# Keys transposed on TensorE instead of by DMA, weight words joined in two VectorE steps, and diagonal copies cut to their 32x32 blocks

## The chip, the cores and the metric

The kernel runs on one core of a Trainium2 chip. The metric is device time in microseconds (us) of one execution; the number to forecast is the median of a few executions of the changed kernel. Five engines work side by side, each through its own list of instructions in a fixed order: TensorE (PE, with its weight loads as PEld), VectorE (DVE), ScalarE (ACT), GpSimd (POOL) and SyncE (SP). SP does no arithmetic here: it issues nearly all transfers, in order, and an instruction of it that waits holds back every transfer behind it.

## The reference

Two stages. First a delta rule with a state of 48x48 per head, over 4 batches, 8 heads and 768 positions:

```python
k_n = k / (np.linalg.norm(k, axis=-1, keepdims=True) + 1e-06)
for t in range(S):
    kt, vt, bt = (k_n[:, :, t], v[:, :, t], beta[:, :, t, None])
    y[:, :, t] = np.einsum('bhd,bhde->bhe', q[:, :, t], state)
    v_old = np.einsum('bhde,bhd->bhe', state, kt)
    state = state + bt[:, :, :, None] * np.einsum('bhd,bhe->bhde', kt, vt - v_old)
```

Then a feed-forward layer over the 3072 tokens of 384 numbers that come out, with 2048 hidden units and a rational function:

```python
h = x @ w_in
P = a[0] + a[1] * h + a[2] * h2 + a[3] * h3          # h2 = h*h, h3 = h2*h
Q = 1.0 + np.abs(b[0]) * np.abs(h) + np.abs(b[1]) * h2
return (P / (Q + 1e-06)) @ w_out
```

`moe_w_in` and `moe_w_out` arrive as 64-bit floating-point numbers, two 32-bit words each.

## The kernel before

The 768 positions are cut into 12 chunks of 64. Within a chunk the recurrence is solved in closed form: products of keys with keys (`pg`), an inverse of a triangular matrix by 16x16 blocks on VectorE (`inverse`), and a solve in four steps (`solve_start`, three `solve_step`). Each of the 12 chunks then gives 256 tokens, and the hidden units are worked through in 8 units of 256 (`hidden`, `numerator`, `quotient`, `accumulate`), so there are 96 units in all. Numbers are split into two 16-bit parts, and a product is three passes over them.

The main loop (L1067) goes over the 96 units; beside unit n it runs one slice of attention: `back` of chunk c+1, `middle` of c+2, `front` of c+3, `ahead` of c+4. So the attention of later chunks is hidden under the units of earlier ones. Ahead of the loop stands a start (L1046): the attention of the first chunks, and the loading and conversion of all weights. A scheduler sets the order on each engine from this program and from the buffers; the order is then fixed.

What the change touches:

- **Weights.** `to_f32` (L387) turns a tile of 64-bit words into 32-bit floats. A transfer brings 128x512 (or 128x384) words into one of nine staging buffers (`wsi`, `wso`); ACT takes the absolute value of the high words (L394, tile `wai` or `wao`); POOL clamps it from both sides (L395); DVE shifts it left by 3 and masks it (L396), joins the sign bits of the high word (L403) and the top three bits of the low word (L403 again). That is done for 24 tiles of `w_in` (256 columns) and 32 of `w_out` (192 columns). For `w_out` the lower clamp on POOL is `gate`, a number that DVE makes at the end of the inverse of chunk 0 (L661), so that these tiles come behind that chunk.
- **Keys.** `keys_normalized` (L565) scales a chunk's keys; `transposed` (L526) splits them on POOL into `kn` (L251, L257). For chunk 0 they are transposed on PE (`ptk`, L547) and copied out by ACT in four pieces (L549). For the other 11 chunks `kn` is written to DRAM (`xdk`, L537) and read back by a transposing transfer (`tk`, L554). `xdk` is also what `knbd` is later filled from (L506). Heads are padded from 48 to 64 rows.
- **Diagonals.** A product for two batches at once takes a block-diagonal operand of 128x128 per head: `kbd`, `qbd`, `knbd`, `wbd`, `ebd`, `mbd`. `to_diagonal` (L500) fills its two 64x64 blocks by two transfers of 64 rows. `wbd` serves two things in turn: the triangle `gl` for the product `pe` (L1003, L677), then the inverse `wc` for the solve (L678), so its second filling (L517) waits until PE has done `pe`.
- **Relays through DRAM.** The key products `g` go out to `gd` (L597) and their 16x16 blocks come back as `gb` (L607); the inverse goes out to `img` (L666) and comes back as `wc` (L670), whole 64x64 squares each.
- **PSUM.** The pool `ps_f` has one buffer, which the products of the front stage (`pg`, `pm`, `pe`, `ptq`, `px` and small ones) take in turn.

## Time and profile before

| | us |
|---|---|
| three runs | 833.64, 830.17, 834.09 (median 833.64) |
| the profiled execution, time | 831.25 |
| its span, first to last instruction | 829.5 |
| mean granted TensorE clock | 0.917 |

The profiled execution is 2.4 us under the median, and its own time is 1.75 us more than its span. Busy times of the engines, and how they change over the span, stand in the prediction. In the rows of groups the columns are: source line, engine, operation, output and inputs, shapes, count, then busy us in all and mean ns of one, then the engine's idle time just before and what ended it. Instructions on DVE overlap by some 0.07 us at their ends, so that a duration of 0.25 costs less than 0.25 where another one follows at once.

### The profile page before, as it was taken

Reading aid. Unit: us, or ns where it says so; the run is one execution under the profiler, and the core shown is the slowest. Engines: PE = TensorE matmul, PEld = TensorE weight load, DVE = VectorE, ACT = ScalarE, POOL = GpSimd, SP = SyncE. Lnnn points to the kernel's source line nnn. Section 1 sums busy time; section 2 is a strip of 40 time slices with the busy share of each in tenths; the row PEclk is TensorE's granted clock in tenths of the full one; section 3 lists DMA queues with packets and bytes.
Section 4 is the critical chain, followed back from the end, with each engine's and each line's share of the span. In section 5 each row is a group of like instructions: output and inputs, shape, how many; then the busy total and the mean of one; then the engine's idle time right before and its main releaser. Section 6 shows DMA issues by size and latency. Waiting matters only on the chain.

```text
span 829.5 us, 23311 instructions
## 1 busy us (share of the span) xinstructions
PE 626.5 (76%) x9466; PEld 498.2 (60%) x9466; DVE 752.7 (91%) x1325; ACT 553.8 (67%) x988; POOL 428.0 (52%) x416
## 2 busy tenths in 40 slices
PE   0320445867779678898887898996988979998995
PEld 0210444656568467677666676775766867876663
DVE  5999899878999789899899998989999998997996
ACT  4756666745757466767686776866767766776773
POOL 8653865424261353573664665736735545353532
PEclk9975565898989899999999999998999999999999
DMA  8999897759865777849979468586676733400000
GB/s 231 239 195 197 203 183 139 131 99 165 140 119 105 124 134 125 143 81 147 140 126 155 79 137 149 87 161 116 105 151 101 129 63 55 78 2 20 1 21 19
DMA packets 430956, 99.42 MB, mean 120 GB/s; under 512 B 408064, under 2 KB 427520, under 8 KB 430848
## 3 DMA queue, kind: packets, MB, share of 16 engines
q1 hardware_dynamic: 428672, 96.77, 63.0%
q8 instruction: 74, 1.21, 0.6%
q10 hardware_dynamic: 2176, 1.17, 0.5%
q14 instruction: 34, 0.28, 0.1%
HBM read 40.47 MB, written 19.94 MB: 73 GB/s over the span
## 4 chain that ended last, share of the span: by engine, by line
DVE 44%; PE 16%; issue 11%; DMA 11%; ACT 7%; SPq 6%; POOL 5%; POOLq 0%; DVEq 0%; ACTq 0%
PE ph L867 6%; PE po L929 5%; DVE mw L909 4%; DVE mu L887 4%; DVE mw L889 4%; DVE mu L891 4%; DVE w_out L403 4%; DVE mg L908 3%; DMA q_b<-in_q_dram 3%; DVE mu L913 2%; POOL mg L914 2%; PE pu L479 1%; DVE mg L906 1%; ACT mu L884 1%; DVE z L259 1%
## 5 line engine op out<-in xcount | busy, mean ns | idle before, releaser
L867 PE MATMUL ph<-xT,w_in 128*128 128x256 f16 x1728 | 222.4, 280 | 20.5 <-DVE mu L891 16.7
L929 PE MATMUL po<-w_out,mg 128*128 128x384 f16 x1152 | 218.5, 333 | 24.2 <-POOL mg L914 22.2
L914 POOL TENSOR_TENSOR mg<-mu,mr 128x512 f16<-128x512 f32 x96 | 132.3, 1378 | 154.4 <-DVE mu L913 99.2
L867 PEld LDWEIGHTS <-w_in 128*128 128x128 f16 x1728 | 169.7, 100 | 58.4 <-DVE mu L891 14.0
L929 PEld LDWEIGHTS <-mg 128*128 128x128 f16 x1152 | 108.6, 100 | 93.6 <-POOL mg L914 29.8
L890 ACT ACTIVATE mw<-mw 128x512 f32<-128x512 f32 x96 | 60.4, 629 | 65.0 <-DVE mw L889 64.8
L884 ACT ACTIVATE mu<-ph,coef,msc 128x512 f32<-128x512 f32 x96 | 73.9, 770 | 33.5 <-PE ph L867 19.7
L909 DVE SCALAR_TENSOR_TENSOR mw<-mw,msc,mg 128x512 f32<-128x512 f32 x96 | 89.9, 937 | 0.6
L887 DVE TENSOR_TENSOR mu<-ph,mu 128x512 f32<-128x512 f32 x96 | 65.4, 681 | 24.2 <-ACT mr L886 13.3
L479 PEld LDWEIGHTS <-kbd 128*128 128x128 f16 x1680 | 60.7, 104 | 26.7 <-issue 15.1
L911 POOL TENSOR_TENSOR mu<-mu,mw 128x512 f32<-128x512 f32 x36 | 49.3, 1370 | 48.4 <-DVE mw L909 34.8
L891 DVE SCALAR_TENSOR_TENSOR mu<-mu,msc,ph 128x512 f32<-128x512 f32 x96 | 70.6, 736 | 0.0
L889 DVE SCALAR_TENSOR_TENSOR mw<-mr,msc,ph 128x512 f32<-128x512 f32 x96 | 70.6, 735 | 0.0
L902 ACT ACTIVATE mr<-mw,msc 128x512 f32<-128x512 f32 x96 | 69.1, 720 | 1.6
L886 ACT ACTIVATE mr<-ph,msc 128x512 f32<-128x512 f32 x96 | 65.2, 679 | 0.0
L479 PE MATMUL pu<-z,ebd 128*128 128x48 f16 x1728 | 51.5, 185 | 15.5 <-DVE z L259 13.7
L479 PEld LDWEIGHTS <-ebd 128*128 128x128 f16 x1728 | 50.8, 98 | 18.9 <-issue 15.5
L903 ACT ACTIVATE mr<-mr 128x512 f32<-128x512 f32 x96 | 60.4, 629 | 1.4
L908 DVE SCALAR_TENSOR_TENSOR mg<-mu,msc,mr 128x512 f16<-128x512 f32 x60 | 56.4, 941 | 4.1 <-ACT mr L903 4.1
L479 PEld LDWEIGHTS <-wbd 128*128 128x128 f16 x1152 | 33.9, 99 | 29.1 <-issue 28.5
L895 POOL TENSOR_SCALAR mu<-mu,msc 128x512 f32<-128x512 f32 x36 | 30.9, 858 | 36.9 <-DVE mu L891 34.8
L913 DVE SCALAR_TENSOR_TENSOR mu<-mu,msc,mw 128x512 f32<-128x512 f32 x60 | 49.2, 820 | 0.4
(211 smaller groups left out, 1228.5 us busy)
## 6 DMA issues: line engine op xcount, KB each, us to landing
wsi<-in_moe_w_in_dram SPq DMA_DIRECT2D x24, 256.0 KB, 4.8
xdk<-kn SPq DMA_DIRECT2D x24, 256.0 KB, 3.9
kbd<-tk SPq DMA_DIRECT2D x24, 256.0 KB, 4.6
gd<-g SPq DMA_DIRECT2D x24, 256.0 KB, 4.2
wso<-in_moe_w_out_dram SPq DMA_DIRECT2D x32, 192.0 KB, 3.7
mbd<-mm SPq DMA_DIRECT2D x24, 256.0 KB, 5.0
wc<-img SPq DMA_DIRECT2D x24, 256.0 KB, 4.6
wbd<-wc SPq DMA_DIRECT2D x24, 256.0 KB, 4.4
```

Source lines behind the costliest of these rows:

```text
L479: nc.tensor.matmul(dst[p][:, h], head(bd, lp, p * H + h), head(rt, rp, p * H + h), start=start and n == 0 and h == 0, stop=stop and n == l ...
L867: nc.tensor.matmul(ph[:, i], w_in[:, f2, wp, cc, i * P : (i + 1) * P], x[:, xp, cc], start=k == 0, stop=k == 3 * NCC - 1,)
L884: nc.scalar.activation(u, ph, AF.Identity, scale=A3, bias=a2)
L887: nc.vector.tensor_mul(u, ph, u)
L889: nc.vector.scalar_tensor_tensor(out=w, in0=z, scalar=B0, in1=ph, op0=ALU.add, op1=ALU.mult)
L891: nc.vector.scalar_tensor_tensor(out=u, in0=u, scalar=A1, in1=ph, op0=ALU.add, op1=ALU.mult)
L902: nc.scalar.activation(r, w, AF.Ln, bias=Q0)
L908: nc.vector.scalar_tensor_tensor(out=g[:, 0], in0=u, scalar=A0, in1=r, op0=ALU.add, op1=ALU.mult)
L909: nc.vector.scalar_tensor_tensor(out=w, in0=w, scalar=Q0, in1=g[:, 0], op0=ALU.add, op1=ALU.mult)
L913: nc.vector.scalar_tensor_tensor(out=u, in0=u, scalar=A0, in1=w, op0=ALU.add, op1=ALU.subtract)
L914: nc.gpsimd.tensor_mul(g[:, 1], u, r)
L929: nc.tensor.matmul(po[p], g[:, gp, i, p * P : (p + 1) * P], w_out[:, f2, wp, i], start=f2 == lo and i == 0 and k == 0, stop=f2 == hi - 1 a ...
```

## The change

1. `to_f32` has no masking step and no clamp. ACT takes the absolute value of the high word times a constant (or times `gate`) as a 32-bit float; POOL makes the bare sign bit straight from the high word (minimum with 0, times 0) and writes it to the target `t`; DVE then joins in two steps: low word shifted right by 29, or `t`; absolute value shifted left by 3, or `t`. `gate` moves from POOL's instruction to ACT's.
2. All chunks' keys are transposed on PE: 16 transposes into one `ps_f` buffer (`pk`), and two ACT copies of 96x1024. `xdk` and the transposing transfer are gone, and `knbd` is filled straight from the split keys in SBUF (now called `nk`). The padding of heads from 48 to 64 is gone, so `kbd`, `qbd` and `tk` have 96 rows instead of 128, in transfers of 48 rows instead of 64.
3. `gd`, `wc` and `wbd` are moved as the two 32x32 blocks on the diagonal of each 64x64 square (four transfers of 32 rows in place of two of 64), `mbd` as the 32-row halves of its triangle (four transfers, two of 128 and two of 64 columns). `wc` becomes one fixed buffer, zeroed once by DVE.
4. The triangle `gl` has a diagonal buffer of its own, `gbd` (DVE zeroes it at the start), without its first 16 rows; it no longer shares with `wbd`.

```diff
-        nc.scalar.activation(a, wh.bitcast(F32), AF.Abs)
-        nc.gpsimd.tensor_scalar(a, a, 3.0e38, keep, op0=ALU.min, op1=ALU.max)
-        nc.vector.tensor_scalar(
-            t, a.bitcast(U32), 3, KEEP, op0=ALU.logical_shift_left, op1=ALU.bitwise_and
-        )
-        for word, scalar, in1, op0, op1 in (
-            (wh, 0xC0000000, t, ALU.bitwise_and, ALU.bitwise_or),
-            (wl, 29, t, ALU.logical_shift_right, ALU.bitwise_or),
-        ):
-            nc.vector.scalar_tensor_tensor(out=t, in0=word, scalar=scalar, in1=in1, op0=op0, op1=op1)
+        nc.scalar.activation(a, wh.bitcast(F32), AF.Abs, scale=bias)
+        nc.gpsimd.tensor_scalar(t.bitcast(F32), wh.bitcast(F32), 0.0, 0.0, op0=ALU.min, op1=ALU.mult)
+        for word, scalar, op0 in ((wl, 29, ALU.logical_shift_right), (a.bitcast(U32), 3, ALU.logical_shift_left)):
+            nc.vector.scalar_tensor_tensor(out=t, in0=word, scalar=scalar, in1=t, op0=op0, op1=ALU.bitwise_or)
...
-                for a in range(HG):
+                for p in PAIRS:
                     nc.sync.dma_start(
-                        out=bd[sl].rearrange("t p i (n a) b d -> t (p i n) a b d", a=HG)[:, :, a, b],
-                        in_=t[:, :, :, :, a, b].rearrange("p i n t d -> t (p i n) d"),
+                        out=bd[sl, p, :, :, b].rearrange("t i n d a -> t (i n) (d a)"),
+                        in_=t[p * C : (p + 1) * C, :, :, b].rearrange("t i n d a -> t (i n) (d a)"),
                     )
...
+            elif nm == "g":
+                sl = slice(b * C + 16, (b + 1) * C)
+                nc.sync.dma_start(out=bd[sl, :, b], in_=t[sl])
             elif nm == "w":
-                nc.sync.dma_start(out=bd[sl, :, b, : t.shape[2]], in_=t[sl])
+                for x in HALVES:
+                    nc.sync.dma_start(out=bd[rows_of(b, x), :, b, x], in_=t[rows_of(b, x), :, x])
             else:
-                nc.sync.dma_start(out=bd[sl, :, :, b, : t.shape[3]], in_=t[sl])
+                for x in HALVES:
+                    nc.sync.dma_start(
+                        out=bd[rows_of(b, x), :, :, b, x.start :], in_=t[rows_of(b, x), :, :, x.start :]
+                    )
...
-        for p in PAIRS:
-            nc.sync.dma_start(
-                out=xd[p].rearrange("i n t a b d -> t (i n) (a b d)"),
-                in_=x[p * C : (p + 1) * C].rearrange("t i (n a) b d -> t (i n) (a b d)", n=NH),
+        pt = ps_f.tile([P, 2, NPAIR, H, C], F16, tag="a", name="p" + nm)[:R]
+        t = sb.tile([R, 2, NPAIR, NH, C, HG], F16, tag="tt", name="t" + nm)
+        for i in range(2):
+            for h in range(H):
+                n, a = divmod(h, HG)
+                nc.tensor.transpose(
+                    pt[:, i, :, h], x[:, i, n, :, :, a].rearrange("p b d -> p (b d)"), ident16
+                )
+            nc.scalar.copy(
+                t[:, i].rearrange("x p n t a -> x (p n) a t"), pt[:, i].rearrange("x p (n a) t -> x (p n) a t", a=HG)
             )
...
-        nc.sync.dma_start(
-            out=t.rearrange("x p i n t a -> x (p i n t a)"),
-            in_=xd.rearrange("p i n t a b d -> (p i n t a) (b d)"),
-            transpose=True,
-        )
...
-            nc.sync.dma_start(out=as_rows(gd, b), in_=g[b * C : (b + 1) * C])
+            for t in HALVES:
+                nc.sync.dma_start(out=as_rows(gd, b)[t, :, t], in_=g[rows_of(b, t), :, t])
...
-            nc.sync.dma_start(out=words[b * C : (b + 1) * C], in_=as_rows(im, b))
+            for t in HALVES:
+                nc.sync.dma_start(out=words[rows_of(b, t), :, t], in_=as_rows(im, b)[t, :, t])
...
-                info[c]["gbd"] = to_diagonal("w", info[c].pop("gl"))
+                info[c]["gbd"] = to_diagonal("g", info[c].pop("gl"))
```

The scheduler's order moves with it. First, VectorE at the first weight tiles. `wai` is what ACT and POOL have made of a tile, `wsi` the tile as it landed, `w_out` the memory in which the float is put together. Before:

```order
L396 TENSOR_SCALAR w_out<-wai_0_790 128x256
L403 SCALAR_TENSOR_TENSOR w_out<-wsi_0_788,w_out 128x256 x2
L396 TENSOR_SCALAR w_out<-wai_1_798 128x256
L403 SCALAR_TENSOR_TENSOR w_out<-wsi_1_796,w_out 128x256 x2
L396 TENSOR_SCALAR w_out<-wai_2_806 128x256
```

And now:

```order
L394 SCALAR_TENSOR_TENSOR w_out<-wsi_0_792,w_out 128x256
L394 SCALAR_TENSOR_TENSOR w_out<-wai_0_794,w_out 128x256
L394 SCALAR_TENSOR_TENSOR w_out<-wsi_1_799,w_out 128x256
L394 SCALAR_TENSOR_TENSOR w_out<-wai_1_801,w_out 128x256
L394 SCALAR_TENSOR_TENSOR w_out<-wsi_2_806,w_out 128x256
```

Three instructions on a tile have become two, and the first of them no longer reads what ACT makes.

Second, SyncE behind the end of the inverse of chunk 0, whose result is `wh` and goes to `img`. Before:

```order
L666 DMA img_147<-wh_383 128x16x16
L554 DMA_TRANSPOSE tk_1558<-xdk_1555 128x2048
L670 DMA wc_388<-img_147 64x16x64 x2
L391 DMA wso_1_1211<-in_moe_w_out_dram 128x384
L391 DMA wso_0_1220<-in_moe_w_out_dram 128x384
```

After seven more tiles of `w_out` there came `kbd`, and only then `wbd`. Now:

```order
L653 DMA img_147<-wh_382 128x16x16
L516 DMA mbd_143<-mm_375 32x16x128
L516 DMA mbd_143<-mm_375 32x16x64
L516 DMA mbd_143<-mm_375 32x16x128
L658 DMA wc_127<-img_147 32x16x32 x4
L513 DMA wbd_139<-wc_127 32x16x64 x4
L516 DMA mbd_143<-mm_375 32x16x64
L388 DMA wso_1_1182<-in_moe_w_out_dram 128x384
```

The next tile of `w_out` (the tenth) now stands behind `wbd`, which waits until `wc` has landed; before, it stood behind `wc` alone.

Third, ScalarE in the main loop, around the square of chunk 8's `v` (`sq_8`). `mu` and `mr` are a unit's first two activations out of PSUM, `mw` its third. Before:

```order
L886 ACTIVATE mr_7557<-ph_7536,msc_6417 128x512
L255 ACTIVATE z_1_7833<-pu_7572,zmask 128x768
L267 ACTIVATE sq_8_7889,fs_7886<-v_7399 128x768
L890 ACTIVATE mw_7506<-mw_7506 128x512
L613 COPY wt_129<-bblk 128x16
```

And now:

```order
L875 ACTIVATE mr_7631<-ph_7610,msc_6521 128x512
L264 ACTIVATE sq_8_8020,fs_8017<-v_7527 128x768
L542 COPY tk_7177<-pk_7176 96x8x2x64
L556 ACTIVATE sq_8286<-k_7754 128x768
L879 ACTIVATE mw_7634<-mw_7634 128x512
L542 COPY tk_7177<-pk_7176 96x8x2x64
```

The two copies out of the new transposes stand between the activations of a unit, one on each side of `mw`.

More of the change, by code (lines that the diff above doesn't have):

```diff
@@ L57 @@
     C = 64
-    DP = 64
+    R = 2 * D
     NB = C // 16
@@ L108 @@
     SRC = {"k": k, "q": q, "v": v}
-    LD_BUFS = {"k": 1, "v": 2}
+    LD_BUFS = {"k": 1, "q": 1, "v": 2}
     loaded = {}
     def load(nm, c):
-        if nm == "q":
-            t = q_b
-        else:
-            t = sb.tile([P, NPAIR * H, D], F32, tag="ld" + nm, name=f"{nm}_{c}", bufs=LD_BUFS[nm])
+        t = sb.tile([P, HP, D], F32, tag="ld" + nm, name=f"{nm}_{c}", bufs=LD_BUFS[nm])
         with behind(nm, c):
@@ L122, in load @@
                 else:
+                    part = t[sl].rearrange("t (h i) d -> t h i d", i=2)
                     for i in range(2):
-                        if nm == "q":
-                            nc.sync.dma_start(out=t[sl, :, i, :D], in_=src[2 * i + b].rearrange("h t d -> t h d"))
-                            continue
-                        nc.sync.dma_start(out=t[sl, i * H : (i + 1) * H], in_=src[2 * i + b].rearrange("h t d -> t h d"))
+                        nc.sync.dma_start(out=part[:, :, i], in_=src[2 * i + b].rearrange("h t d -> t h d"))
         loaded[nm, c] = t
-    q_b = cpool.tile([P, H, 2, DP], F32, name="q_b")
-    nc.vector.memset(q_b[..., D:], 0.0)
     identf = cpool.tile([P, P], F32, name="identf")
@@ L217 @@
             nm + "bd",
-            eng=nc.vector if nm in "kwe" else nc.gpsimd,
+            eng=nc.vector if nm in "kweg" else nc.gpsimd,
         )
@@ L240, in as_rows, with rows_of @@
         )
+    HALVES = [slice(i * C // 2, (i + 1) * C // 2) for i in range(2)]
+    def rows_of(b, t):
+        return slice(b * C + t.start, b * C + t.stop)
     def as_blocks(ap):
         return ap[:, : 16 * C].rearrange("m (i s) -> m i s", s=C)[:, :, :16]
-    S16 = cpool.tile([P, HP, D], F32, name="S16")
+    S16 = cpool.tile([R, HP, D], F32, name="S16")
     def split16(dst, src, scale=None, eng=None, hi=None):
@@ L457, in head @@
         elif t.shape[3] == NH and t.shape[-1] == HG:
-            t = t[:, p, part, h // HG, ..., h % HG]
+            t = (t[:, p, part] if t.shape[-2] == D else t[:, part, p])[:, h // HG, ..., h % HG]
         elif t.shape[2] == HP:
             t = t[:, part, m]
-        elif t.shape[3] == H:
-            t = t[:, p, part, h]
         else:
@@ L476, in mm3p @@
     def mm3p(dst, bd, rt, p, start=True, stop=True):
+        out = R if bd is diag["kn"][0] else 2 * (C - 16) if bd is diag["g"][0] else P
+        rows = R if any(bd is t for t in diag["q"] + diag["k"]) else P
         for n, (lp, rp) in enumerate(PASSES):
@@ L479, in mm3p @@
                 nc.tensor.matmul(
-                    dst[p][:, h],
-                    head(bd, lp, p * H + h),
-                    head(rt, rp, p * H + h),
+                    dst[p][:out, h],
+                    head(bd, lp, p * H + h)[:rows],
+                    head(rt, rp, p * H + h)[:rows],
                     start=start and n == 0 and h == 0,
@@ L524, in grouped, with transposed @@
         return t.rearrange("p (g a) x -> p g a x", a=HG)
-    def transposed(x, src, nm, soon):
+    def transposed(src, nm):
+        x = sb.tile([P, 2, NH, 2, D, HG], F16, tag="kn", name="n" + nm, bufs=3)
         split16(
-            [x[:, i, :, :, :D].rearrange("p h b d -> p b h d") for i in range(2)],
-            src.rearrange("p (b h) d -> p b h d", b=2),
+            [x[:, i].rearrange("p n b d a -> p n a (b d)") for i in range(2)],
+            src.rearrange("p (n a b) d -> p n a (b d)", a=HG, b=2),
             eng=nc.gpsimd,
@@ L684, in off_blocks @@
                 sl = slice(b * C + 16 * j, b * C + 16 * j + 16)
-                nc.sync.dma_start(out=ebd[sl, :, :, b, 16 * (j + 1) :], in_=et[sl, :, :, 16 * j :])
+                src = slice(sl.start - 16 * b, sl.stop - 16 * b)
+                nc.sync.dma_start(out=ebd[sl, :, :, b, 16 * (j + 1) :], in_=et[src, :, :, 16 * j :])
     def scales(c):
@@ L721, in queries_transposed @@
                 nc.tensor.transpose(
[L722 removed]
+                    pt[:, p, h // HG, :, h % HG], qt[sl, 2 * h : 2 * h + 2].rearrange("x b d -> x (b d)"), identf[sl, sl]
                 )
[L724 removed]
+        split16(parts(t), pt, d["sq"][:R])
     def diagonals(c):
@@ L791, in state_next @@
             nc.vector.scalar_tensor_tensor(
-                out=by_pair(S16), in0=pd[2], scalar=d["isv"], in1=by_pair(S16), op0=ALU.mult, op1=ALU.add
+                out=by_pair(S16), in0=pd[2][:R], scalar=d["isv"][:R], in1=by_pair(S16), op0=ALU.mult, op1=ALU.add
             )
         else:
-            nc.scalar.activation(by_pair(S16), pd[2], AF.Copy, scale=d["isv"])
+            nc.scalar.activation(by_pair(S16), pd[2][:R], AF.Copy, scale=d["isv"][:R])
     def outputs(c):
```

57 lines of the change are left out of this document (21 added, 36 removed).

## The prediction

> **What bounds the kernel now.** I read the page's busy times first, then a table by stage, then the groups by shape, the waits, and VectorE's instructions in order of time where the weights are converted. The page's first part, over the whole span:
>
> ```profile
> PE 626.5 (76%) x9466; PEld 498.2 (60%) x9466; DVE 752.7 (91%) x1325; ACT 553.8 (67%) x988; POOL 428.0 (52%) x416
> ```
>
> DVE is busy for 752.7 of 829.5 us: removing all its idle time could give 77 us, and all else must come out of its work. To see where the idle time lies, I cut the span into stages: up to the first weight tile, up to `gate`, up to the first unit, the first units, the main loop, the last units without attention. The two rows of the last block of this fence give the cuts at 72 and 148 us. In the table the columns are the stretch, its length, then busy us (and instructions) of PE, PEld, DVE, ACT, POOL, the granted clock, the share of DMA and GB/s.
>
> ```profile
> 0.00:20.00 20.00, 2.04 (x16) 1.72 (x17) 10.48 (x16) 7.69 (x17) 17.01 (x42) 1.00 0.82 227
> 20.00:72.00 52.00, 13.63 (x140) 10.14 (x139) 50.92 (x138) 34.81 (x85) 26.69 (x34) 0.79 0.94 217
> 72.00:148.00 76.00, 31.96 (x596) 28.94 (x596) 69.85 (x217) 48.98 (x134) 49.85 (x68) 0.61 0.85 171
> 148.00:220.00 72.00, 53.35 (x824) 43.29 (x825) 62.91 (x122) 44.18 (x76) 26.00 (x22) 0.88 0.80 140
> 220.00:720.00 500.00, 432.97 (x6986) 346.95 (x6984) 465.22 (x706) 345.32 (x562) 263.77 (x216) 0.96 0.68 118
> 720.00:829.00 109.00, 92.51 (x913) 67.17 (x908) 93.36 (x134) 72.82 (x118) 44.64 (x36) 1.00 0.05 12
> ...
> L661 DVE TENSOR_SCALAR gate<-wt x1: 147/147/147, 71.9 to 71.9; 128x1 uint32<-128x1 uint32 x1
> 147.94 0.69 DVE L887 TENSOR_TENSOR mu<-ph,mu 128x512 f32<-128x512 f32 x1 [2.15 <-ACT mr L886]
> ```
>
> From 20 to 148 us DVE works 120.8 of 128 us: in the weights, what DVE no longer does is time won, unless something else ends last there. The nearest is DMA, busy for 0.94 and 0.85 of those stretches. From 148 to 720 us DVE idles 9.1 + 34.8 = 43.9 us; there a saving must come from what it waits for. The last 109 us hold no attention, and nothing in them changes.
>
> **The masking step.** These groups are what DVE does to the weights, and the instructions under them show two tiles without and one with POOL beside it:
>
> ```profile
> L396 DVE TENSOR_SCALAR w_out<-wai 128x256 uint32<-128x256 uint32 x24 | 9.9, 421 | 4.7 <-POOL wai L395 4.7
> L396 DVE TENSOR_SCALAR w_out<-wao 128x192 uint32<-128x192 uint32 x28 | 10.6, 381 | 0.6 <-POOL wao L395 0.6
> L396 DVE TENSOR_SCALAR wo<-wao 128x192 uint32<-128x192 uint32 x4 | 1.0, 261 | 0.0
> L403 DVE SCALAR_TENSOR_TENSOR w_out<-wsi,w_out 128x256 uint32<-128x256 uint32 x48 | 25.8, 558 | 0.2
> ...
> 29.02 0.28 DVE L396 TENSOR_SCALAR w_out<-wai 128x256 uint32<-128x256 uint32 x1
> 29.22 0.41 DVE L403 SCALAR_TENSOR_TENSOR w_out<-wsi,w_out 128x256 uint32<-128x256 uint32 x1
> ...
> 77.52 0.25 DVE L396 TENSOR_SCALAR w_out<-wao 128x192 uint32<-128x192 uint32 x1
> 77.69 0.76 DVE L403 SCALAR_TENSOR_TENSOR w_out<-wso,w_out 128x192 uint32<-128x192 uint32 x2
> ...
> 86.06 1.52 DVE L396 TENSOR_SCALAR w_out<-wao 128x192 uint32<-128x192 uint32 x1 [0.61 <-POOL wao L395]
> ...
> 85.99 1.47 POOL L581 TENSOR_TENSOR k<-k,nrm 128x768 f32<-128x768 f32 x1
> ```
>
> The 56 instructions of L396 go; the two joins stay, and I price the one that now reads `wai` like the one it replaces. Undisturbed, a masking step costs 0.20 us from start to start at 256 columns and 0.17 at 192: 24 x 0.20 + 32 x 0.17 = 10.2 us. As measured, with the stretched ones (1.52 us beside POOL's 1.47), it is 9.9 + 10.6 + 1.0 = 21.5 us, less the overlap of 0.08 us on each (0.28 to 0.20), 56 x 0.08 = 4.5: 17.0 us. The difference is stretch beside POOL. L403 stretches too: 0.41 us alone, 0.558 on average, so some of that stretch will pass to the instruction that takes the place. I take 14, about the middle.
>
> The Trainium skill (GPSIMD Engine Reference, section Key points) says that POOL shares its SBUF interfaces with VectorE, in contention with DVE instructions that run in a 2-port mode or have two SBUF inputs. The trace agrees for both forms, by the stretched 1.52 us and by the 0.558 against 0.41. By that rule the whole stretch passes on, the joins having two inputs, and the term would be 10.2 in place of 14.
>
> **The start and the tenth tile.** DVE's first masking step waited 4.72 us for POOL's clamp, which waited for ACT and stood behind the keys of chunk 0. POOL's new step needs only the landed tile, so DVE can begin sooner: between 0 and 4.7 us, I take 2, because the tiles that follow still have to land.
>
> ```profile
> 18.55 0.48 DVE L396 TENSOR_SCALAR w_out<-wai 128x256 uint32<-128x256 uint32 x1 [4.72 <-POOL wai L395]
> ...
> img<-wh SPq DMA_DIRECT2D x12, 128.0 KB, 3.7
> wc<-img SPq DMA_DIRECT2D x24, 256.0 KB, 4.6
> wso<-in_moe_w_out_dram SPq DMA_DIRECT2D x32, 192.0 KB, 3.7
> wbd<-wc SPq DMA_DIRECT2D x24, 256.0 KB, 4.4
> ebd<-et SPq DMA_DIRECT2D x24, 48.0 KB, 3.4
> tk<-xdk SPq DMA_TRANSPOSE x11, 5.3
> xdk<-kn SPq DMA_DIRECT2D x24, 256.0 KB, 3.9
> ...
> L554 SPq DMA_TRANSPOSE tk<-xdk x11: 2152/2773/4797, 73.0 to 610.4; - x11
> L537 SPq DMA_DIRECT2D xdk<-kn x24: 595/634/2911, 18.1 to 600.1; - x24
> ```
>
> Against that stands SP behind `gate`. Nine tiles of `w_out` lie staged then; the tenth can be asked for only as they are freed, and SP now has `wbd` ahead of it, which waits for `wc`. Counted from the end of the inverse, with 0.63 us an issue (`xdk`'s median): `img` lands at 3.7; the fourth `wc` is issued by 6.2 and lands at 10.8; the fourth `wbd`, the last `mbd` and the tile take 1.9, the tile 3.7 more: 16.4 us. Before it was 3.7, two `wc` 1.3, the tile 0.6 + 3.7: 9.3 us. So 7.1 us later, with DVE's nine staged tiles and the first scalings of `w_out` as cover. Queued behind that wait on SP are all further weight tiles; DVE waits for them. Of the 7.1 I charge 3 (bounds 0 and 7.1). The other moves there (chunk 0's `kbd` behind 21 tiles in place of 10, the zeroing of `wc` and `gbd` in the first 20 us, where DVE idles 9.5) I cost at nothing: DVE is busy with tiles meanwhile. If chunk 0's inverse became the last thing, they would cost up to the 9 us of eleven more tiles at two joins of 0.41 us each.
>
> `gate` also adds a wait on ACT: its absolute values of `w_out` tiles used to run ahead of `gate`, POOL's clamp waited.
>
> ```profile
> L394 ACT ACTIVATE wao<-wso 128x192 f32<-128x192 f32 x32 | 11.4, 367 | 7.4 <-DVE w_out L396 5.5 <-DMA wso<-in_moe_w_out_dram 1.8
> ```
>
> Behind it in ACT's list stand more such values and the squares of the same tiles, which DVE must join first; so I cost it at nothing, and at nine staged tiles, 9 x 0.367 = 3.3 us, if DVE stood waiting for them at once. The bound of 7.1 holds that, as these values run while the tenth tile is fetched.
>
> **The main loop.** Three terms. ACT takes 22 more copies of 96x1024 in the 11 chunks, PE 176 more transposes:
>
> ```profile
> L549 ACT COPY tk<-ptk 128x512 f16<-128x512 f16 x4 | 2.7, 734 | 0.6 <-PE ptk L547 0.6
> L547 PE MATMUL ptk<-ident,kn 128*128 128x128 f16 x16 | 2.0, 308 | 17.8 <-POOL kn L251 16.4 <-ACT tk L549 1.4
> ...
> ACT mw L890 <- DVE mw L889: 64.8, 54, 4.7
> ACT sq L267 <- DMA q_b<-in_q_dram: 19.7, 7, 7.3
> ACT sq L267 <- DMA v<-in_v_dram: 10.6, 4, 3.3
> ACT sq L570 <- DMA k<-in_k_dram: 6.1, 3, 2.8
> ...
> SPq L517 <- PE pe L479: 19.7, 4, 11.9
> ```
>
> A copy of twice the size is at most 2 x 0.734 = 1.47 us, so at most 22 x 1.47 = 32.3 us of ACT. Between 220 and 720 us ACT idles 155 of 500, and 64.8 of its waits are for DVE's own `mw`, next to which the copies stand in the new order; what hides them is that wait. Uncovered they cost all 32.3; I charge 3. PE's transposes are at most 176 x 0.308 = 54 us by their modelled ends, in a PE that is busy for 433 of 500; I charge 1, as PE may be two units ahead (`ph` has two PSUM buffers). In the other direction, SP and DMA. ACT waited 36.4 us for inputs (19.7 + 10.6 + 6.1), loads that SP issues late. SP loses, per chunk, the transposing issue (2.77), two `xdk` (1.27) and its share of the wait for `pe` (19.7 / 12 = 1.6), now that `gbd` is a separate buffer: 5.7 us. It gains eight issues, 5.0 us, and a wait of `wbd` on `wc` that other issues used to fill. So SP wins little, but each chunk's keys skip 3.9 and 5.3 us of transfers, and 0.68 of DMA share comes down. Of DVE's 43.9 us idle I give back 10; the bounds are 0 and the 36.4 us of those waits. The loop's sum: 10 - 3 - 1 = 6 us won.
>
> The Trainium skill (DMA: Bandwidth & Descriptors, section Rules for kernel authors) says of two transfers to disjoint halves of the partitions not to bother, because they serialize, and of transfers under 64 KB that one mostly pays overhead. The rows above agree in kind: 48 KB landed in 3.4 us where 256 KB took 4.4. By that rule the split of `gd`, `wc`, `wbd` and `mbd` brings only issues, and the loop's term would be 6 - 5 = 1.
>
> **The sum.** 14 + 2 - 3 + 6 = 19 us from a span of 829.5: 810.5, and 812.3 with the 1.75 us around it. The profiled run lies 2.4 under its median, so I forecast **815 us**.
>
> **The rivals.** First, the loop gains more: DVE's waits there go down to a third, 29 us in place of 6, the total is 42 and the time 792. For it: the 36.4 us of ACT's waits for loads, and the removal of the one transfer that holds SP longest. Against: SP's balance of 5.7 against 5.0.
>
> Second, transfers bound the start. The weights are as many bytes as before, and DMA was busy 0.94 and 0.85. Then DVE's 14 + 2 turn into waits for tiles, 6 - 3 = 3 us remain, and the time is 831, no change. Against: DVE hardly ever waited for L403's tiles (0.2 us of idle in its row), and `xdk`, `tk` and a quarter of the rows of `kbd` leave those stretches.
>
> Third, slower: PE and ACT hold each other at the transposes. The second eight transposes may start only when ACT has copied out the first, a copy stands in ACT's list behind a unit's activation, and behind the transposes in PE's list stand the solve and the next unit's `ph`. A hold is a copy and an activation ahead of it (L549's 1.47 and as much as half of that again, 2.2 us), two to a chunk in 11 chunks: 48 us. If all of it reached DVE, with the start's 13 and the 10 of the transfers won: 829.5 + 48 - 23 + 4.1 = 859. It decides from 23 us on, that is if half of each hold gets past the two units that PE is ahead. Against: the new order puts other work of PE between the two eights, and PE idles 67 us between 220 and 720.
>
> **How the numbers follow.** My forecast 0.62, the first rival 0.16, the second 0.14, the third 0.08. About 0.5% (829.5 to 837.8 us) is what a measurement can tell from no change. The forecast and the first rival are faster, of the second 0.05; so faster 0.83, same 0.09, slower 0.08. The range: with 10.2, 0, 7.1 and 1 the sum is 4 us, 830; with 17, 4.7, 0 and 15 it is 37, 797; of the loop's wider bounds the rest is in the first and third rival. I take 797 to 832, which leaves out the third rival and half of the first, 0.16.
>
> **What would show it.** Right: two instructions a tile on DVE with means like L403's, the first unit's `mu` near 135 us, `gate` within some us of 72, DVE's idle from there to 720 us a little under 44. Wrong: L394 rows well above 0.56 us (the stretch passed on), a DVE wait of over 7 us for a `wso` tile behind `gate`, DVE idle at `mu` behind PE `pk` or ACT `tk` adding up to more than 20 us, or idle time in the loop cut to a third.

## The result and the profile after

| | before | after |
|---|---|---|
| median of 10 runs of each, us | 832.57 (829.50 to 834.14) | 838.82 (835.91 to 841.35) |
| ratio, 95% interval | | 1.0071 (1.0052 to 1.0091) |
| the profiled execution: time, span | 831.25, 829.5 | 836.76, 835.0 |

The forecast was 815, in a range of 797 to 832, with 0.08 for slower. The changed kernel is slower by 0.7%, more than the 0.5% that a measurement can tell.

The first part of the page of after, over the whole span:

```profile
PE 659.2 (79%) x9642; PEld 531.0 (64%) x9642; DVE 733.2 (88%) x1270; ACT 573.6 (69%) x1008; POOL 456.9 (55%) x415
```

DVE has lost 55 instructions and 19.5 us of work (752.7 to 733.2), as much as the whole forecast gain, and the span has grown by 5.5 us: DVE stands idle for 25 us more. PE has 32.7 us more work, of which the prediction expected the transposes alone.

The table by stage of after, cut at its own `gate` and first `mu`, with those two rows behind it (columns as in the prediction):

```profile
0.00:20.00 20.00, 0.00 (x0) 0.10 (x1) 13.24 (x16) 6.45 (x14) 14.27 (x38) 1.00 0.81 231
20.00:74.40 54.40, 15.95 (x156) 11.62 (x155) 51.46 (x129) 36.50 (x87) 48.49 (x42) 1.00 0.68 164
74.40:150.80 76.40, 40.99 (x638) 37.59 (x639) 60.28 (x165) 54.39 (x133) 51.40 (x57) 0.68 0.68 135
150.80:220.00 69.20, 53.95 (x916) 44.35 (x915) 60.76 (x120) 43.77 (x77) 31.43 (x28) 0.91 0.56 88
220.00:720.00 500.00, 447.29 (x6892) 362.02 (x6891) 446.60 (x701) 351.87 (x569) 261.06 (x215) 0.96 0.45 77
720.00:835.00 115.00, 100.98 (x1051) 75.28 (x1047) 100.85 (x143) 80.59 (x130) 50.22 (x40) 0.99 0.09 21
...
L648 DVE TENSOR_SCALAR gate<-wt x1: 141/141/141, 74.4 to 74.4; 128x1 uint32<-128x1 uint32 x1
150.82 0.69 DVE L876 TENSOR_TENSOR mu<-ph,mu 128x512 f32<-128x512 f32 x1 [2.46 <-ACT mr L875]
```

`gate` comes at 74.4 us (71.9 before), the first `mu` at 150.8 (147.9 before; forecast near 135). From `gate` to `mu` DVE idles 16.1 of 76.4 us (6.2 of 76.0 before), from 220 to 720 us 53.4 of 500 (34.8 before). DMA fell from 0.68 to 0.45 of the main loop, and DVE waits more there all the same. Of the signs that the prediction named, the joins' means (589 and 557 ns at 256 columns) and `gate` came out as it said, and no wait of DVE at the joins was longer than 1.3 us; the first `mu` and DVE's idle time did not.

For the comparisons below I cut every run in two: the **start**, up to the first `mu`, and the **loop**, the rest. Before, then after:

```profile
0.00:147.90 147.90, 47.63 (x752) 40.80 (x752) 131.19 (x365) 91.38 (x235) 93.44 (x143) 0.72 0.88 195
147.90:829.50 681.60, 578.83 (x8714) 457.40 (x8714) 621.55 (x960) 462.42 (x755) 334.51 (x274) 0.96 0.59 104
```

```profile
0.00:150.80 150.80, 56.94 (x794) 49.31 (x795) 124.97 (x308) 97.33 (x234) 114.16 (x135) 0.84 0.70 158
150.80:835.00 684.20, 602.23 (x8850) 481.65 (x8848) 608.21 (x962) 476.23 (x774) 342.72 (x281) 0.96 0.40 69
```

At the start DVE works 6.2 us less and idles 25.8 instead of 16.7; in the loop it works 13.3 us less and idles 76.0 instead of 60.1.

### The profile page after: what moved, and what is told of

It is laid out like the page before. It is cut to its first block, busy times and chain, and to the rows that moved or that the text cites. A ratio compares the mean times of both kernels' runs of the same rounds, so it can differ in the third digit from the quotient of the medians.

```text
span 835.0 us, 23732 instructions
## 1 busy us (share of the span) xinstructions
PE 659.2 (79%) x9642; PEld 531.0 (64%) x9642; DVE 733.2 (88%) x1270; ACT 573.6 (69%) x1008; POOL 456.9 (55%) x415
## 4 chain that ended last, share of the span: by engine, by line
DVE 31%; PE 25%; ACT 14%; DMA 10%; issue 9%; SPq 6%; POOL 4%; POOLq 0%; ACTq 0%; DVEq 0%
PE ph L856 7%; PE po L918 7%; DVE mw L898 3%; DVE mu L876 3%; DMA q<-in_q_dram 3%; DVE mw L878 3%; DVE mu L880 2%; DVE w_out L394 2%; PE pu L470 2%; DVE mg L897 2%; ACT mu L873 2%; POOL mg L903 2%; PE pd L470 2%; DVE pr L632 2%; PE pg L470 2%
## 5 line engine op out<-in xcount | busy, mean ns | idle before, releaser
L918 PE MATMUL po<-w_out,mg 128*128 128x384 f16 x1152 | 225.5, 341 | 31.2 <-POOL mg L903 23.7
L856 PE MATMUL ph<-xT,w_in 128*128 128x256 f16 x1728 | 219.5, 278 | 9.7 <-DVE mu L880 7.0
L918 PEld LDWEIGHTS <-mg 128*128 128x128 f16 x1152 | 111.3, 102 | 105.0 <-POOL mg L903 29.8
L898 DVE SCALAR_TENSOR_TENSOR mw<-mw,msc,mg 128x512 f32<-128x512 f32 x96 | 87.4, 910 | 0.6
L876 DVE TENSOR_TENSOR mu<-ph,mu 128x512 f32<-128x512 f32 x96 | 65.5, 683 | 17.6 <-ACT mr L875 12.4
L470 PEld LDWEIGHTS <-kbd 96*128 96x128 f16 x1680 | 58.6, 101 | 10.7 <-DMA kbd<-tk 5.7
L897 DVE SCALAR_TENSOR_TENSOR mg<-mu,msc,mr 128x512 f16<-128x512 f32 x60 | 53.9, 900 | 6.6 <-ACT mr L892 6.6
L470 PEld LDWEIGHTS <-ebd 128*128 128x128 f16 x1728 | 51.4, 98 | 9.7 <-issue 6.9
L902 DVE SCALAR_TENSOR_TENSOR mu<-mu,msc,mw 128x512 f32<-128x512 f32 x60 | 52.9, 881 | 0.4
L470 PE MATMUL pe<-wc,gbd 128*96 128x48 f16 x576 | 29.9, 208 | 28.3 <-DMA wc<-img 23.5
L470 PEld LDWEIGHTS <-gbd 128*96 128x96 f16 x576 | 29.5, 130 | 29.1 <-issue 29.1
```

Source lines behind the costliest of these rows:

```text
L470: nc.tensor.matmul(dst[p][:out, h], head(bd, lp, p * H + h)[:rows], head(rt, rp, p * H + h)[:rows], start=start and n == 0 and h == 0, sto ...
L856: nc.tensor.matmul(ph[:, i], w_in[:, f2, wp, cc, i * P : (i + 1) * P], x[:, xp, cc], start=k == 0, stop=k == 3 * NCC - 1,)
L876: nc.vector.tensor_mul(u, ph, u)
L897: nc.vector.scalar_tensor_tensor(out=g[:, 0], in0=u, scalar=A0, in1=r, op0=ALU.add, op1=ALU.mult)
L898: nc.vector.scalar_tensor_tensor(out=w, in0=w, scalar=Q0, in1=g[:, 0], op0=ALU.add, op1=ALU.mult)
L918: nc.tensor.matmul(po[p], g[:, gp, i, p * P : (p + 1) * P], w_out[:, f2, wp, i], start=f2 == lo and i == 0 and k == 0, stop=f2 == hi - 1 a ...
```

## The experiments

Four questions: do narrower operands on PE cost the time; what is the joining worth; how much of all this is the order of the queues; and does the third rival's hold of PE and ACT exist. Ratios are to the kernel before, on the same chip, with 95% intervals. The runs come from several chips, on which the kernel before took 830.1 to 832.6 us, so that two kernels are compared by their ratios and not by their microseconds.

**Narrower operands.** In after the operands `knbd` and `gbd` are loaded into PE as 96 columns; before they had 128. e1_wide makes them 128 wide again:

```diff
-        "kn": [P, NPAIR, 2, NH, 2, D, HG],
+        "kn": [P, NPAIR, 2, NH, P, HG],
...
-        "g": [P, HP, 2, C - 16, 2],
+        "g": [P, HP, P, 2],
...
-                    dst[p][:out, h],
+                    dst[p][:, h],
```

e8_room has the same two larger shapes and keeps `[:out]`, so that it has the memory of e1_wide and uses 96 columns:

```diff
-                    head(bd, lp, p * H + h)[:rows],
+                    head(bd, lp, p * H + h)[:rows, :out],
```

> The changed kernel with 128 columns again in the two products whose stationary tiles it had cut to 96 (pe from gbd, pd from knbd); the 32 added columns are zeros and nothing else is edited, though the scheduler orders the program anew. Theory W (a stationary tile of 96 columns is loaded more slowly than one of 128): the load and matmul rows of pe and pd go from about 50 ns of busy time each (28.6 and 29.5 us of loading, 29.0 and 29.9 us of matmul) back to about 30, PE's busy time falls by 20 to 25 us, and since PE stands on about a quarter to a half of the chain of waits the time falls by 5 to 12 us below the changed kernel, to 827-834. Rival T (PE and ACT hold each other at the transposes of the keys): PE's busy time may fall, but the time stays within 3 us of the changed kernel's 839. Rival O (what counts is the new order of the program, whichever edit caused it): the time moves by several us, up or down, and the control with 96 columns in the same room moves as far.

> The control to the run before it: the same larger tiles for gbd and knbd, cleared over 128 columns, but only the first 96 are loaded and multiplied, as in the changed kernel. Theory W: the load rows of gbd and knbd stay near 130 ns and 29 us each, and the time stays near the changed kernel's 839 (835 to 843). Rival O: the time moves as far as with 128 columns, since the order changes here too.

e1_wide: 832.38 us, 1.0007 (0.9981 to 1.0033). e8_room: **820.76 us, 0.9860 (0.9822 to 0.9899)**. The kernel that runs the very same 96-column operations as after is 2% faster than after; the wide one, meant as the cure, gains less. More room for a tile made the scheduler draw all its queues anew: 4311 of the 9616 instructions that the program puts on PE and 492 of DVE's 1270 stand at another place. So neither run is a test of one edit until the order is held.

The load itself did get slower, as the instructions of the matmul's line by tile show (min/median/max ns, first and last start, shape). After:

```profile
L470 PEld LDWEIGHTS <-kbd x1680: 96/97/291, 41.8 to 725.5; 96*128 96x128 f16 x187
L470 PEld LDWEIGHTS <-gbd x576: 121/123/196, 82.1 to 704.5; 128*96 128x96 f16 x192
L470 PEld LDWEIGHTS <-knbd x528: 121/123/193, 114.0 to 714.2; 128*96 128x96 f16 x176
```

e1_wide:

```profile
L469 PEld LDWEIGHTS <-gbd x576: 96/97/117, 82.0 to 702.1; 128*128 128x128 f16 x192
L469 PEld LDWEIGHTS <-knbd x528: 96/97/119, 107.7 to 708.7; 128*128 128x128 f16 x176
```

96 columns take 123 ns, 128 columns 97; 96 rows by 128 columns (`kbd`) take 97 too, so it is the columns. The Trainium skill (TensorE: Matmul & The Clock Gate, section Weight-path perf modes — Fast Weight Load (FWL) and DoubleRow) says that the fast load is on when there are 128 weights and the type is not FP32; these rows agree with it.

**The joining.** e2_join is the kernel before with change 1 alone, e3_nojoin is after without it.

```diff
-        nc.vector.tensor_scalar(
-            t, a.bitcast(U32), 3, KEEP, op0=ALU.logical_shift_left, op1=ALU.bitwise_and
-        )
...
+        nc.gpsimd.tensor_scalar(t.bitcast(F32), wh.bitcast(F32), 0.0, 0.0, op0=ALU.min, op1=ALU.mult)
+        for word, scalar, op0 in ((wl, 29, ALU.logical_shift_right), (a.bitcast(U32), 3, ALU.logical_shift_left)):
+            nc.vector.scalar_tensor_tensor(out=t, in0=word, scalar=scalar, in1=t, op0=op0, op1=ALU.bitwise_or)
```

> The kernel before with the two-step joining of the weights alone (no masking step on DVE, the sign bit made on POOL). The prediction's sum of the start: the first unit's subtraction moves from 147.9 us to about 135 and the time falls by 12 to 16 us, to 817-821. Rival S (the start is a chain of chunk 0's solve and chunk 1's inverse through all engines and not a sum of DVE's work): the last join ends some 15 us earlier, the first unit's subtraction moves by less than 4 us, and the time falls by 0 to 5 us, to 828-833.

> The changed kernel with the three-step joining of the kernel before, so that only the keys on PE, the blocks and the diagonal of its own are left. If the joining is worth 14 us by itself: 850-855. Rival S: the first unit stays within 4 us of 150.8 and the time within 5 us of the changed kernel's 839; then all that the change loses lies in the parts that are left here.

e2_join: 838.15 us, 1.0070 (1.0047 to 1.0093). e3_nojoin: 834.08 us, 1.0023 (1.0000 to 1.0046). By these two, taking 56 instructions from the fullest engine costs half a per cent or more; both were ordered anew. Neither time that was expected of e2_join came. Its first `mu` does come earlier, at 141.2 us, but its loop, in which no weight is joined, takes 692.2 us instead of 681.6.

**The order held.** To part an edit from the order that it brings, I chained the instructions of each engine by dependencies that only fix the order of issue and wait for nothing.

```diff
+        for a, b in zip(row, row[1:]):
+            tc.add_manual_dep(
+                traced[e][b],
+                traced[e][a].name,
+                mybir.DependencyInfo(mybir.DependencyClass.NoSync, mybir.DependencyReason.DATA),
+                reason="pinned",
+            )
```

p1_order is the changed kernel, unchanged, in the order of e8_room. p3_wide_e8order is e1_wide in that order; p4_wide_afterorder is e1_wide in the order of after. p2_join is the two-step joining in the order of before, every new instruction at the place of the one that it replaces; for that the sign bits have a tile of their own (`sg`), and ACT doesn't wait for `gate`.

> The changed kernel, instruction for instruction (96 columns, small tiles), with each engine's queue pinned to the order that the scheduler chose for the control with the larger tiles. Theory O (the order of the queues decides): the control's time, 818 to 824, with the first unit near 145 us and DVE idle in the loop near the control's. Rival R (the larger tiles themselves, their clearing or their addresses made the control faster): the changed kernel's 836 to 841.

> The kernel before with the two-step joining, every engine's queue pinned to the order of the kernel before, the 56 masking instructions taken out of DVE's. So that this order can hold, the sign bits get a small tile of their own, ACT's tile has four buffers instead of three, and ACT's step does not wait for the gate. The prediction's sum: first unit about 13 us earlier, 816 to 821. Rival S (DVE's work does not bound the start): DVE waits longer where the masks stood, the first unit moves by less than 4 us, 828 to 833.

> 128 columns for pe and pd, queues pinned to the order of the control with 96: what the width alone costs in that order. Theory W: PE's busy time falls by some 20 us (pe and pd each from about 50 ns a load to 30), the time by 3 to 8 us below the control's 820.8, to 813-818. If PE's slower loads hide behind DVE in this order: within 2 us of 820.8.

> The same 128 columns in the order of the changed kernel. Theory W: 3 to 8 us below its 838.8, 831 to 836. If hidden: 837 to 841. Either way the gap of some 18 us between the two orders should stay with the order and not with the width.

| | us | ratio |
|---|---|---|
| p1_order | 820.65 | 0.9872 (0.9844 to 0.9900) |
| p3_wide_e8order | 822.48 | 0.9898 (0.9870 to 0.9926) |
| p4_wide_afterorder | 834.19 | 1.0034 (1.0013 to 1.0056) |
| p2_join | 827.19 | 0.9948 (0.9924 to 0.9971) |

The changed kernel, with the same instructions and the same tiles, takes 838.8 us in one order and 820.7 in another, by the ratios 2.0% or some 17 us apart. The width is worth nothing in the faster order and about 0.4% in after's own, by intervals that just overlap. And the joining, at before's own places, is a gain of 0.5%, where e2_join had called it a loss of 0.7%.

p1_order, cut in two, and its first `mu`:

```profile
0.00:145.30 145.30, 54.75 (x735) 47.67 (x736) 122.84 (x299) 95.49 (x231) 111.72 (x133) 0.84 0.68 159
145.30:819.30 674.00, 601.10 (x8909) 482.95 (x8907) 611.89 (x972) 479.10 (x778) 351.27 (x283) 0.96 0.41 71
...
145.27 0.69 DVE L876 TENSOR_TENSOR mu<-ph,mu 128x512 f32<-128x512 f32 x1 [3.29 <-ACT mr L875]
```

Against after, 5.5 us of the difference lie in the start and 10.2 in the loop. DVE's work is the same within 2 us in all (733.2 and 734.7); its idle time is not: 62.1 us in the loop instead of 76.0.

**How far the order alone goes.** One small memset, moved from POOL to DVE, changes the work by 1 us at most (0.3 us of POOL for the first, 1.0 for the second, in before's trace) and makes the scheduler draw all its queues again. In each of the two kernels (b of before, c of after) two variants, the first edit for b1_clear and c1_clear, the second for b2_zero and c2_zero:

```diff
-    wt_b = zeroed(1, [P, 272], F32, "wt")
+    wt_b = zeroed(1, [P, 272], F32, "wt", eng=nc.vector)
...
-    nc.gpsimd.memset(zero, 0.0)
+    nc.vector.memset(zero, 0.0)
```

> The kernel before, with one clearing of a tile (wt, 272 columns, at the start) moved from POOL to DVE, and the scheduler left to order the program again: nearly the same work in another order. Theory O (any edit draws a new order, and the order is worth 10 to 20 us either way): a time up to 15 us off 831, on either side. Rival I (the order matters little to this kernel, and the 18 us between the two orders of the changed kernel are an accident of its own): 829 to 833.

> The changed kernel with the same clearing moved from POOL to DVE, ordered anew. Theory O: anywhere from 818 to 842. If the change itself costs time: 836 to 842 again.

> The kernel before, with another clearing (the 1040 zeros for the images in DRAM) moved from POOL to DVE, ordered anew. Theory O: a third time for the same work, up to 15 us off 831. Rival I: 829 to 833.

> The changed kernel with that other clearing moved from POOL to DVE, ordered anew. Theory O: anywhere from 818 to 842. If the change is a gain that one order hid, the three orders of the changed kernel that were not chosen for their time lie below the three of the kernel before on the mean, by up to 10 us.

| | median us | ratio | start | loop |
|---|---|---|---|---|
| before | 832.57 | 1 | 147.9 | 681.6 |
| b1_clear | 829.14 | 0.9971 (0.9950 to 0.9992) | 146.8 | 678.8 |
| b2_zero | 827.37 | 0.9956 (0.9934 to 0.9979) | 151.4 | 672.8 |
| after | 838.82 | 1.0071 (1.0052 to 1.0091) | 150.8 | 684.2 |
| c1_clear | 836.16 | 1.0049 (1.0020 to 1.0077) | 155.8 | 674.5 |
| c2_zero | 842.21 | 1.0122 (1.0085 to 1.0158) | 165.5 | 676.3 |
| p1_order | 820.65 | 0.9872 (0.9844 to 0.9900) | 145.3 | 674.0 |

The moved memset of b1_clear gave 7052 of the 9440 instructions that the program puts on PE another place. Start and loop are those of one profiled execution each. By the ratios, three orders of the kernel before span 0.44% (some 4 us), four of the changed one 2.5% (21 us). The means of the ratios are 0.9976 and 1.0029, half a per cent apart, about what before's orders span. On average the changed kernel starts later (154.3 us against 148.7) and loops equally long (677.3 against 677.7).

One of the four is not a fresh draw: p1_order's order was taken over because it was fast. The other three all lie above the three of before, at 1.0081 on the mean. So what was expected if one order had hidden a gain, that they lie below, did not come; left to the scheduler, these draws speak for a loss of about 1%. Three draws a side are few.

**The third rival.** h1_before_order is after with the queues of DVE and PE in the order of before (the transposes where the scheduler likes). h2_keys_before_order is the change without the joining, with the queues of DVE, PE, ACT and POOL in before's order; only transposes, copies and transfers are free. h3_wide_before_order is h1 with 128 columns. f1_third_buffer is after in its own order with a third buffer for the transposed keys:

```diff
-        t = sb.tile([R, 2, NPAIR, NH, C, HG], F16, tag="tt", name="t" + nm)
+        t = sb.tile([R, 2, NPAIR, NH, C, HG], F16, tag="tt", name="t" + nm, bufs=3)
```

(and the same for `tq`, which shares the buffers).

> The changed kernel with DVE's and PE's queues pinned to the order of the kernel before (the 56 masks dropped; the keys' 16 transposes a chunk fall where the scheduler puts them; ACT, POOL and SP ordered by it too). If the prediction's sum holds for an order that stays (-3.6 as measured for the joining, -6 for the rest): 819 to 823. If the parts themselves cost time (rival C: PE, ACT and the 96 columns), 832 to 842.

> The change without the joining (three steps as before), with DVE's, PE's, ACT's and POOL's queues pinned to the order of the kernel before, the transposes and copies of the keys and all transfers placed by the scheduler. The prediction's terms for these parts: 3 at the start, -6 in the loop, so 826 to 830. Rival C: 833 to 840, with the loss either in the start (chunk 0's keys later) or in the loop (PE and ACT waiting for each other).

> As the first of these four, with 128 columns in pe and pd. Theory W: 2 to 6 us below it. If PE's slower loads are hidden there as in the order of the control: within 2 us of it.

> The changed kernel in its own order, with three instead of two buffers for the transposed keys and queries, so that ACT's copy of the keys need not wait until the queries of two chunks before have left the buffer. Theory B (that wait of 4.7 us, with PE's 3.0 and DVE's 4.4 behind it, is part of the loss): 833 to 836. If it is hidden: 837 to 841.

h1: 907.18 us, 1.0927 (1.0892 to 1.0961). h2: **867.70 us, 1.0456 (1.0420 to 1.0493)**. h3: 893.45 us, 1.0747 (1.0713 to 1.0781). f1: 834.08 us, 1.0056 (1.0027 to 1.0085), not told apart from after's 1.0071; its 834 us lie in the range of theory B, but before was faster on that chip too (830.8). h1 and h2 lie far above both ranges that were set for each, and h3 is further below h1 than theory W said. PE's waits in h2, and then two of DVE's (us in all, times, the longest):

```profile
PE pg L477 <- DMA kbd<-tk: 21.9, 3, 8.2
PE pk L546 <- ACT tk L549: 21.7, 10, 4.4
PE px L818 <- ACT tk L549: 11.0, 6, 2.7
```

```profile
DVE S L787 <- PE pd L477: 15.1, 4, 11.3
DVE xs L819 <- PE px L818: 14.4, 6, 4.0
```

In after there are fewer of them, and one wait of ACT's own copy:

```profile
PE pk L539 <- ACT tk L542: 8.6, 4, 3.3
...
ACT tk L542 <- DMA qbd<-tq: 4.7, 1, 4.7
```

So PE and ACT do hold each other at the transposes, for 2.2 us a time, if the other work stays where it was: 21.7 us in 10 holds between the two eights. Six times PE's `px` waits for the copies as well, 11.0 us. DVE waits for `px` as often in h2, 14.4 us; in before it has no such wait, nor one for `pd`. Of the longer span of h2, 10.7 us lie in the start and 24.5 in the loop. The scheduler moves other work between, and in after 8.6 us in 4 holds are left. One of them in after's timeline, in order of time, shows how a hold travels:

```profile
335.10 1.33 SPq L503 DMA_DIRECT2D qbd<-tq  x2
...
339.48 1.30 ACT L542 COPY tk<-pk 96x1024 f16<-96x1024 f16 x1 [4.69 <-DMA qbd<-tq]
...
340.83 1.01 PE L539 MATMUL pk<-ident,nk 128*96 128x128 f16 x8 [3.02 <-ACT tk L542]
...
343.43 0.63 ACT L892 ACTIVATE mr<-mr 128x512 f32<-128x512 f32 x1
...
344.16 2.40 DVE L895 TENSOR_TENSOR mg<-mu,mr 128x512 f16<-128x512 f32 x1 [4.38 <-ACT mr L892]
```

ACT's copy waits 4.69 us for a buffer that the filling of `qbd` still reads, PE's second eight transposes wait 3.02 for the copy, and the unit's `mr`, queued on ACT behind the copy, reaches DVE 4.38 us late. In f1_third_buffer that wait of ACT is gone, and the place is lost anyway:

```profile
336.39 1.30 ACT L542 COPY tk<-pk 96x1024 f16<-96x1024 f16 x1
...
343.00 1.37 ACT L250 CAST mm<-m 128x1024 f16<-128x1024 f32 x1 [4.07 <-DMA mbd<-mm]
344.23 0.62 ACT L892 ACTIVATE mr<-mr 128x512 f32<-128x512 f32 x1
...
344.95 2.39 DVE L895 TENSOR_TENSOR mg<-mu,mr 128x512 f16<-128x512 f32 x1 [4.81 <-ACT mr L892]
```

Another instruction ahead of `mr` in ACT's queue now waits, for another transfer, and DVE waits as long.

The last two take the hold itself away: all sixteen transposes first, then the two copies. k1_one_round is h2 with that edit; k2_one_round_fast is p1_order with it.

```diff
         for i in range(2):
             for h in range(H):
...
-            nc.scalar.copy(
+        for i in range(2):
+            nc.scalar.copy(
```

> The change without the joining, queues pinned to the order of the kernel before as in h2, but all sixteen transposes of a chunk's keys are given out before the two copies, so that PE no longer waits for ACT's first copy between the two eights. Theory C (PE and ACT hold each other there): PE's 21.7 us of waiting at pk go, the time falls from 867.7 by 10 to 25 us, to 843-858. Rival K (what costs there is that the keys come late to their products in that order, through PE's and ACT's queues at all): 862 to 870.

> The changed kernel with the same edit, queues pinned to the order of the control with the larger tiles (820.7), the transposes and copies of the keys placed by the scheduler. Theory C: there PE waited 3.4 us at pk and 1.9 at px for the copies, so 817 to 820. Rival K: 820 to 823.

k1: 854.83 us, 1.0266 (1.0230 to 1.0302). k2: 826.56 us, 0.9933 (0.9899 to 0.9966). PE's waits in k1 have none of `pk` for `tk` any more:

```profile
PE pk L546 <- POOL nk L249: 19.0, 1, 19.0
PE px L819 <- ACT tk L550: 14.4, 6, 5.1
```

The 21.7 us of waits are gone and the time falls by 12.9 (by the ratios 15.8): that is what these holds cost there, a third or a little more of h2's 37 us. The edit also moved some of ACT's copies and SP's transfers against each other. The other 24 are not explained by it; `px` still waits for the copies, 14.4 us. In the fast order the same edit did not help: 826.6 us, where it should have been no slower than 820.7. This loss is not firm, as five of k2's twelve executions took 820.4 to 821.8 us and seven 825.8 to 832.2.

## Why the prediction was wrong, step by step

**The masking, -14.** The 56 instructions went, as forecast; the time did not. p2_join, where the order is before's own, shows it alone. Its stages, cut at 20 us, near `gate` and at its first `mu`, and its groups:

```profile
0.00:20.00 20.00, 2.05 (x16) 1.72 (x17) 9.84 (x14) 7.77 (x17) 17.34 (x40) 1.00 0.81 227
20.00:72.00 52.00, 13.48 (x140) 9.93 (x139) 49.30 (x124) 35.75 (x91) 42.83 (x39) 0.64 0.98 223
72.00:144.10 72.10, 33.53 (x596) 30.11 (x596) 63.59 (x174) 47.10 (x129) 58.01 (x65) 0.57 0.86 177
...
L400 DVE SCALAR_TENSOR_TENSOR w_out<-wsi,sgi 128x256 uint32<-128x256 uint32 x24 | 15.7, 663 | 5.3 <-POOL sgi L395 5.3
...
L395 POOL TENSOR_SCALAR sgi<-wsi 128x256 f32<-128x256 f32 x24 | 27.8, 1179 | 0.0
```

DVE's work up to the first `mu` falls from 131.2 to 122.7 us (9.84 + 49.30 + 63.59), by 8.5. The masks' 21.5 us are gone, but the joins take 57.9 us instead of 51.4 (the first join of 256 columns, 558 ns before, takes 663). That leaves 15.0, of which some 5 had been overlap between neighbours, and DVE's other instructions took 1.3 us more. Of the 8.5, DVE's idle time takes back 4.7 (16.7 to 21.4): 3.8 us are left, `mu` at 144.1. The term was 14. Two things were wrong in it. The joins took over nearly all of the stretch, 6.5 of the 6.8 us between 17.0 and 10.2, where I took about half. And POOL's new step I priced at nothing.

**POOL's step, the term that was missing.** The sign bit of 256 columns takes POOL 1.10 us, the clamp that it replaces 0.40 undisturbed (medians 1.10 and 0.45); POOL's work up to the first `mu` rose from 93.4 us to 118.2 in p2_join. And POOL splits the keys of chunk 0, on which `gate` hangs. Before, POOL's keys, then its clamps:

```profile
16.39 1.64 POOL L257 TENSOR_TENSOR kn<-k,kn 128x768 f16<-128x768 f32 x1
...
24.28 0.40 POOL L395 TENSOR_SCALAR wai<-wai 128x256 f32<-128x256 f32 x1 [0.70 <-ACT wai L394]
...
28.04 1.16 PE L479 MATMUL pg<-tk,kbd 128*128 128x64 f16 x18
```

After, the same on POOL and then on PE:

```profile
22.01 1.08 POOL L248 TENSOR_SCALAR nk<-k 128x768 f16<-128x768 f32 x1
23.02 8.10 POOL L392 TENSOR_SCALAR w_out<-wsi 128x256 f32<-128x256 f32 x7
31.09 1.99 POOL L254 TENSOR_TENSOR nk<-k,nk 128x768 f16<-128x768 f32 x1
...
33.13 1.09 PE L539 MATMUL pk<-ident,nk 128*96 128x128 f16 x8
...
41.76 0.45 PE L470 MATMUL pg<-tk,kbd 96*128 96x64 f16 x5 [3.40 <-DMA kbd<-tk]
```

Seven sign bits stand between the two halves of one split; it ends at 33.1 us instead of 18.0, and the first `pg` comes at 41.8 instead of 28.0. The chunk's slack hid most of that (`gate` +2.5 us). In c2_zero it did not. There 32 of POOL's sign bits stand ahead of the second half of the split:

```profile
56.00 1.90 POOL L254 TENSOR_TENSOR nk<-k,nk 128x768 f16<-128x768 f32 x1
...
89.55 0.15 DVE L648 TENSOR_SCALAR gate<-wt 128x1 uint32<-128x1 uint32 x1
```

`gate` comes 17.6 us later than before and the first `mu` at 165.5, 17.5 later. So of the bound that I set for chunk 0's inverse, 9 us, the place was right, the engine and the size were not. In after the last join of the weights ends at 121 us, 18 us earlier than before (139), and the first unit is still later: the joins no longer set the end of the start. ACT still works on tiles of `w_out` there, on the last of them between the first unit's `mu` and `mr`.

**The first step, -2, and the tenth tile, +3.** Within their bounds. DVE's first weight step begins at 17.3 us instead of 18.55, but its second tile no earlier than before (19.96 and 19.94). After's tenth tile behind `gate`, on SP, then before's:

```profile
83.89 5.71 SPq L388 DMA_DIRECT2D wso<-in_moe_w_out_dram  x10
```

```profile
77.81 1.34 SPq L391 DMA_DIRECT2D wso<-in_moe_w_out_dram  x1
```

It is asked for 9.5 us after `gate` instead of 5.9, 3.6 later. What DVE lost by that was not measured by itself.

**The loop, -6.** Not borne out. After's loop is 2.6 us longer than before's. In its three other orders it is 5.3 to 7.6 us shorter, which looks like the forecast; but before's own loop comes out 2.8 and 8.8 us shorter when a memset moves. No gain shows above that spread. DMA's share did come down (from 0.59 to 0.40 of the loop). But the 10 us were to come out of ACT's waits for its loads, and these fell by a fifth only: 37.5 us before (the prediction's 36.4 and another 1.1 for `k`), 30.3 in after (`q` 20.1, `k` 4.6 and 4.2, `v` 1.4). After's longest:

```profile
ACT sq L264 <- DMA q<-in_q_dram: 20.1, 9, 4.1
```

Faster p1_order has the same 20.1 for `q`. And the 4 us that I charged for copies and transposes were 13 in h2, by the holds alone.

**PE's width, not seen at all.** The prediction read the padding's end as a matter of transfers. It makes the loads of `pe` and `pd` slower, and their matmuls too (203 ns each, 183 with 128 columns); that is worth nothing to 0.4% in the two orders that were held on all engines. From h1 to h3 the time falls by 1.6% (1.0927 to 1.0747), but there ACT's queue was free, and 195 of its 1008 instructions stand at another place; so this is not the width alone.

**The third rival, 0.08.** Its mechanism and its 2.2 us a hold were right. Its 48 us were not: in h2, where the work around the transposes stays, PE is held 10 times between the eights and not 22, and those holds cost 13 us; the waits of `px` for the copies, which the rival did not name, come on top. The new order of after cut them to 4; that was the argument against this rival, and it held.

**The steps that failed.** The prediction took work that DVE no longer does for time won. DVE lost 19.5 us of work and gained 25 of idle time. Term by term, the masking's 14 us were 3.7 with the order held (830.85 to 827.19 us), because the joins took over the stretch and DVE's idle time grew by 4.7, (the prediction had priced POOL's new step at nothing); the transposes, charged at 4, cost 13 in h2 by their holds alone; and of the 10 that the loads were to give, no run shows any. On top of that, each term was worked out on before's order and added as if the order stayed, so that a new order was priced at nothing too. The scheduler draws every queue again for any edit, and that alone is worth 2.0% (some 17 us) on the changed kernel, about as much as the whole forecast of 2.2%. The forecast of 815 describes no order that I measured; the best is 820.7, and that one was not drawn for this kernel.

What the edits as such are worth depends on the order: held in before's, the joining gains 0.5% and the rest of the change loses 4.6%; in the order taken from e8_room the set gains 1.3%; in its own three draws it loses 0.5 to 1.2%. Which waits make up after's 0.7% was not shown.

**Open.** Why e8_room's order is the better one: DVE's additional 14 us of waiting (76.0 against p1_order's 62.1) in after's loop are spread over many small waits, and no single one was shown to carry it. The 24 us of h2's loss that are not the holds (DVE's waits for `px` and `pd` are among them, but no run takes them away), the difference between h1 and h2 (h1 has the joining, and ACT and POOL free), and whether k2 loses anything were not settled.

## What to carry to other kernels

Where a scheduler plans the queues, measure a neutral edit or two first: the spread of those times is the least that an edit must move before it counts, and here it was 0.4% for the one kernel and 2.5% for the other, against a forecast of 2.2%. To judge an edit, hold the order and change only it; to ship one, try several orders of it. And price what an edit gives to the engine that seems idle: on POOL stood the keys on which `gate` hung.
